# The first transfers of a retention-and-feed-forward kernel in another order: first weight piece behind two batches, one score and four state sums at other steps

**Chip, cores, metric.** One core of a Trainium2 chip. The metric is the device time of one execution in microseconds (us), the median of its runs.

## The reference

Retention over 4 batches, 8 heads, 768 steps and 64 dimensions, then a two-layer feed-forward block with leaky ReLU, all in fp32:

```python
state = gamma * state + einsum('bhd,bhe->bhde', k[:, :, t], v[:, :, t])
y[:, :, t] = scale * einsum('bhd,bhde->bhe', q[:, :, t], state)
...
h = x @ w_in            # x: 3072 x 512, w_in: 512 x 2048
g = np.maximum(0.01 * h, h)
return g @ w_out
```

The weights come as 64-bit words: ScalarE takes the powers of two out of a piece of 0.5 MB ("powers"), VectorE joins them with the mantissas in three operations ("mantissas"). Only then can TensorE multiply with that piece.

## The kernel before

The kernel works in chunks of 128 tokens of each of four batches. For chunk 0 each batch needs: its q/k (0.5 MB), scored by TensorE and masked by VectorE; its values v (0.25 MB), weighted by decays; the product of both ("values"); and VectorE's "taken", which writes x. `direct(...)` then multiplies x with the first four weight pieces in four steps. Fillers (`keep_busy`) are matmuls whose results nobody reads. Cut to what the change touches:

```python
load_qk(0, 0)
nc.sync.dma_start(out=dec[:, rates:], in_=decay[:, rates:])
load_piece(0)
load_qk(0, 1)
load_v(0, 0)
load_v(0, 1)
nc.sync.dma_start(out=dec[:, :rates], in_=decay[:, :rates])
load_piece(1)
load_qk(0, 2)
load_v(0, 2)
load_piece(2)
load_piece(3, ...)
load_qk(0, 3)
load_v(0, 3)
# ...
keep_busy(7)
score(0, 0)
masked(0, 0)
decay_v(0, 0)            # GpSimd
next_powers()
keep_busy(8)
score(0, 1)
masked(0, 1)
decay_v(0, 1)            # GpSimd
keep_busy(3)
values(0, 0)
next_mantissas()
values(0, 1)
taken(0, 0, x)
taken(0, 1, x)
next_powers()
keep_busy(3)
steps = direct(0, 0, x, parts[0][1], 0)
next(steps)              # first product with weights
score(0, 2)
next_mantissas()
# ... masked, decay_v(0, 2, nc.scalar), powers 2 and 3
next(steps)              # second product
# ... values(0, 2), score(0, 3), next(steps)
values(0, 3)
sums0 = two_banks("sums0")
first_state(0, sums0)
first_state(1, sums0)
# ... half of the next direct, then first_state(2), (3), first_states_taken
```

## Time and profile before

| | before |
|---|---|
| median of 6 runs, us | 671.26 (670.68 to 671.58) |
| span of the profiled run, us | 669.4 |
| TensorE busy | 661.8 us, 99% |
| first product with weights starts | 14.89 us |
| second product starts | 17.85 us |
| next chunk's first score starts | 30.45 us |
| first output product ("A_o") starts | 62.45 us |

The last four rows are starts in the time-ordered instructions of TensorE. From the first product on TensorE has no gap, so these starts are the measure: a start that moves earlier by some tenth moves the end by as much.

### The profile page before, as it was taken

Reading aid. Unit: us, or ns where it says so; the run is one execution under the profiler, and the core shown is the slowest. Engines: PE = TensorE matmul, PEld = TensorE weight load, DVE = VectorE, ACT = ScalarE, POOL = GpSimd, SP = SyncE. Lnnn points to the kernel's source line nnn. Section 1 sums busy time; section 2 is a strip of 40 time slices with the busy share of each in tenths; the row PEclk is TensorE's granted clock in tenths of the full one; section 3 lists DMA queues with packets and bytes.
Section 4 is the critical chain, followed back from the end, with each engine's and each line's share of the span. In section 5 each row is a group of like instructions: output and inputs, shape, how many; then the busy total and the mean of one; then the engine's idle time right before and its main releaser. Section 6 shows DMA issues by size and latency. Waiting matters only on the chain.

```text
span 669.4 us, 10422 instructions
## 1 busy us (share of the span) xinstructions
PE 661.8 (99%) x4517; PEld 573.9 (86%) x4517; DVE 368.3 (55%) x563; ACT 174.2 (26%) x319; POOL 21.4 (3%) x23
## 2 busy tenths in 40 slices
PE   7999999999999999999999999999999999999997
PEld 4888888888888888888888888888888888888886
DVE  4878769889889675414642623553531444331342
ACT  4754456255252002210301310210211220221210
POOL 1000000000000111000000100100100000000000
PEclk9999999999999999999999999999999999999999
DMA  8922222321411553003002200301300000000001
GB/s 323 401 81 95 69 88 64 94 95 63 158 64 64 189 190 127 1 0 112 17 16 80 95 0 1 126 1 64 126 1 0 2 0 34 29 1 1 0 1 63
DMA packets 16028, 49.16 MB, mean 73 GB/s; under 512 B 1904, under 2 KB 2160, under 8 KB 15984
## 3 DMA queue, kind: packets, MB, share of 16 engines
q1 hardware_dynamic: 15984, 48.51, 20.6%
q8 instruction: 35, 0.57, 0.4%
q14 instruction: 9, 0.07, 0.0%
HBM read 42.21 MB, written 6.29 MB: 72 GB/s over the span
## 4 chain that ended last, share of the span: by engine, by line
PE 97%; DMA 1%; DVE 0%; issue 0%; SPq 0%; DVEq 0%
PE B_o L389 12%; PE A_o L389 12%; PE C_o L389 12%; PE C_h L389 12%; PE B_h L389 12%; PE A_h L389 11%; PE D_o L389 6%; PE D_h L389 6%; PE d L411 4%; PE ap L165 3%; PE yp L193 3%; PE yp L184 2%; PE yp L208 1%; DMA qk<-in_qk_dram 1%; PE sums L208 0%
## 5 line engine op out<-in xcount | busy, mean ns | idle before, releaser
L389 PE MATMUL A_h<-x,w 128*128 128x256 f32 x352 | 83.2, 379 | 0.0
L389 PEld LDWEIGHTS A_h<-x,w 128*128 128x128 f32 x352 | 66.9, 190 | 9.1
L389 PE MATMUL A_o<-g,w 128*128 128x256 f32 x288 | 68.0, 379 | 0.0
L424 ACT ACTIVATE g<-g 128x512 f32<-128x512 f32 x66 | 40.2, 630 | 86.9 <-DVE g L338 86.9
L389 PEld LDWEIGHTS A_o<-g,w 128*128 128x128 f32 x288 | 54.7, 190 | 7.4
L429 ACT COPY m<-A_h 128x512 f32<-128x512 f32 x22 | 12.8, 583 | 139.4 <-PE A_h L389 100.5
L338 DVE TENSOR_TENSOR m<-m,B_o 128x512 f32<-128x512 f32 x16 | 11.0, 685 | 65.9 <-PE B_o L389 65.9
L338 DVE TENSOR_TENSOR m<-m,B_h 128x512 f32<-128x512 f32 x22 | 15.1, 686 | 56.8 <-PE B_h L389 56.8
L232 DVE TENSOR_TENSOR x<-yp,dec 128x512 f32<-128x512 f32 x24 | 16.4, 688 | 47.9 <-PE yp L208 35.6
L389 PE MATMUL C_h<-t,w 128*128 128x256 f32 x176 | 42.2, 383 | 0.0
L389 PE MATMUL B_h<-x,w 128*128 128x256 f32 x176 | 42.2, 383 | 0.0
L389 PE MATMUL B_h<-t,w 128*128 128x256 f32 x176 | 41.6, 379 | 0.0
L389 PE MATMUL C_h<-x,w 128*128 128x256 f32 x176 | 41.6, 379 | 0.0
L389 PE MATMUL D_h<-t,w 128*128 128x256 f32 x176 | 41.6, 379 | 0.0
L170 DVE TENSOR_TENSOR am<-ap,mask 128x1024 f32<-128x1024 f32 x24 | 28.6, 1221 | 16.1 <-PE ap L165 16.1
L389 PEld LDWEIGHTS C_h<-t,w 128*128 128x128 f32 x176 | 32.9, 190 | 5.3 <-issue 1.0
L389 PEld LDWEIGHTS B_h<-t,w 128*128 128x128 f32 x176 | 33.4, 190 | 4.5
L389 PEld LDWEIGHTS C_h<-x,w 128*128 128x128 f32 x176 | 33.4, 190 | 4.5
L389 PEld LDWEIGHTS D_h<-t,w 128*128 128x128 f32 x176 | 33.4, 190 | 4.5
L389 PEld LDWEIGHTS B_h<-x,w 128*128 128x128 f32 x176 | 32.9, 190 | 4.9 <-issue 0.3
L147 POOL TENSOR_TENSOR kv<-kv,dec 128x512 f32<-128x512 f32 x18 | 20.9, 1165 | 461.9 <-DMA kv<-in_kv_dram 263.6
L341 DVE TENSOR_TENSOR gd<-g,gd 128x512 f32<-128x512 f32 x48 | 34.7, 723 | 1.8
(109 smaller groups left out, 1056.2 us busy)
## 6 DMA issues: line engine op xcount, KB each, us to landing
raw<-in_weights_dram SPq DMA_DIRECT2D x31, 512.0 KB, 3.9
qk<-in_qk_dram SPq DMA_DIRECT2D x19, 512.0 KB, 4.4
kv<-in_kv_dram SPq DMA_DIRECT2D x17, 512.0 KB, 5.0
out_dram<-o SPq DMA_DIRECT2D x23, 256.0 KB, 2.1
in<-in_qk_dram SPq DMA_DIRECT2D x3, 512.0 KB, 7.2
in<-in_kv_dram SPq DMA_DIRECT2D x3, 512.0 KB, 7.8
kv<-in_kv_dram SPq DMA_DIRECT2D x4, 256.0 KB, 7.5
o_in<-in_qk_dram SPq DMA_DIRECT2D x2, 512.0 KB, 8.4
```

Of the source, the lines that this page charges most:

```text
L147: engine.tensor_tensor(out=v, in0=v, in1=gk.unsqueeze(2).to_broadcast([128, H, D]), op=ALU.mult)
L165: nc.tensor.matmul(ps[ts(u, 64), j, a, :], lhsT=x[ts(j, 64), 1, a, ts(u, 64)], rhs=x[ts(j, 64), 0, a, :])
L170: nc.vector.tensor_tensor(out=am.rearrange("p j a t -> p (j a) t"), in0=scores[c, b].rearrange("p j a t -> p (j a) t"), in1=mask.unsqueeze ...
L184: nc.tensor.matmul(ps[ts(i, 64), j, m, :], lhsT=st[b][ts(j, 64), a, :], rhs=x[ts(j, 64), 0, a, :], start=(m == 0), stop=False, skip_group_ ...
L193: nc.tensor.matmul(ps[ts(i, 64), j, m, :], lhsT=y[:, 1, 2 * a + j, :], rhs=am[:, j, a, :], start=(c == 0 and m == 0), stop=True, skip_grou ...
L232: nc.vector.tensor_tensor(out=blocks, in0=ps[:, :, 0 : HP // 2, :], in1=gq, op=ALU.mult)
L338: nc.vector.tensor_tensor(out=out, in0=a, in1=b, op=ALU.add)
L341: nc.vector.tensor_tensor(out=out, in0=a, in1=b, op=ALU.subtract)
L389: nc.tensor.matmul(half, lhsT=block(w, sa)[:, k, ts(i, 128)], rhs=rhs[:, k, :], start=(first and (i == 0 or split) and n == 0 and k == 0), ...
L411: nc.tensor.matmul(banks[r][:, i, :], lhsT=block(2 * u, r + 2 * kh)[:, k, ts(i, 128)], rhs=x[:, 2 * kh + th, k, :], start=(step == 0 and i ...
L424: nc.scalar.activation(g[:, i], g[:, i], AF.Prelu, alpha=0.01)
L429: nc.scalar.copy(out=got["m1"], in_=ps)
```

## The change

Intent: the q/k and values of the first two batches get in front of the first weight piece, so that more of TensorE's useful work fits into the time before the first product; the two decays of these batches go from GpSimd to VectorE; the third batch's score moves ahead of the first product; the four state sums come together.

```diff
     load_qk(0, 0)
     nc.sync.dma_start(out=dec[:, rates:], in_=decay[:, rates:])
+    load_v(0, 0)
+    load_qk(0, 1)
+    nc.sync.dma_start(out=dec[:, :rates], in_=decay[:, :rates])
+    load_v(0, 1)
     load_piece(0)
-    load_qk(0, 1)
-    load_v(0, 0)
-    load_v(0, 1)
-    nc.sync.dma_start(out=dec[:, :rates], in_=decay[:, :rates])
-    load_piece(1)
     load_qk(0, 2)
     load_v(0, 2)
+    load_piece(1)
     load_piece(2)
 ...
-    decay_v(0, 0)
-    next_powers()
-    keep_busy(8)
+    decay_v(0, 0, nc.vector)
+    keep_busy(6)
     score(0, 1)
+    values(0, 0)
     masked(0, 1)
-    decay_v(0, 1)
+    decay_v(0, 1, nc.vector)
     keep_busy(3)
-    values(0, 0)
+    next_powers()
+    taken(0, 0, x)
+    values(0, 1)
+    taken(0, 1, x)
+    next_powers()
     next_mantissas()
-    values(0, 1)
-    taken(0, 0, x)
-    taken(0, 1, x)
-    next_powers()
+    score(0, 2)
     keep_busy(3)
     steps = direct(0, 0, x, parts[0][1], 0)
     next(steps)
-    score(0, 2)
     next_mantissas()
+    decay_v(0, 2, nc.scalar)
 ...
+    sums0 = two_banks("sums0")
+    for b in range(B):
+        first_state(b, sums0)
     next_mantissas()
     load(1, 3)
     values(0, 3)
-    sums0 = two_banks("sums0")
-    first_state(0, sums0)
-    first_state(1, sums0)
 ...
     taken(0, 3, x)
+    first_states_taken(sums0)
 ...
-    first_state(2, sums0)
-    first_state(3, sums0)
-    first_states_taken(sums0)
```

The diff is cut to transfers and calls; the bookkeeping of tiles in the helper of the state sums moved with them. ScalarE's own order does not change by this: the third batch's decays stood between the powers of pieces 1 and 2 before as well.

More of the change, by code (lines that the diff above doesn't have):

```diff
@@ L212, in first_state @@
     def first_state(b, ps):
-        y = heads.pop((0, b))[1]
+        y = heads[0, b][1]
         sp = ps[:, b // 2].rearrange("p a t -> p (a t)")[:, ds(b % 2 * HP * D, HP * D)]
@@ L220, in first_states_taken @@
     def first_states_taken(ps):
+        for b in range(B):
+            heads.pop((0, b))
         flat = ps.rearrange("p j a t -> p (j a t)").rearrange("p (ba d) -> p ba d", d=D)
@@ L606 @@
     masked(0, 0)
-    decay_v(0, 0)
-    next_powers()
-    keep_busy(8)
-    score(0, 1)
-    masked(0, 1)
-    decay_v(0, 1)
-    keep_busy(3)
-    values(0, 0)
-    next_mantissas()
+    decay_v(0, 0, nc.vector)
+    keep_busy(6)
+    score(0, 1)
+    values(0, 0)
+    masked(0, 1)
+    decay_v(0, 1, nc.vector)
+    keep_busy(3)
+    next_powers()
+    taken(0, 0, x)
     values(0, 1)
-    taken(0, 0, x)
     taken(0, 1, x)
     next_powers()
+    next_mantissas()
+    score(0, 2)
     keep_busy(3)
@@ L622 @@
     next(steps)
-    score(0, 2)
     next_mantissas()
+    decay_v(0, 2, nc.scalar)
     load(1, 2, unit_tile(LATE[0], "in12"))
     masked(0, 2)
-    decay_v(0, 2, nc.scalar)
     next_powers()
@@ L633 @@
     score(0, 3)
-    decay_v(0, 3, nc.scalar)
     taken(0, 2, x)
     masked(0, 3)
+    decay_v(0, 3, nc.scalar)
     next(steps)
+    sums0 = two_banks("sums0")
+    for b in range(B):
+        first_state(b, sums0)
     next_mantissas()
```

## The prediction

> **What bounds the kernel now.** I read the page first (busy shares and the slices), then the chain that ended last in order of time, then the time-ordered instructions of TensorE, of VectorE and ScalarE and of the DMA-issuing queue over the first 35 us, and the waits of TensorE after the start. The page:
>
> ```profile
> span 669.4 us, 10422 instructions
> PE 661.8 (99%) x4517; PEld 573.9 (86%) x4517; DVE 368.3 (55%) x563; ACT 174.2 (26%) x319; POOL 21.4 (3%) x23
> ...
> PE   7999999999999999999999999999999999999997
> ...
> PEclk9999999999999999999999999999999999999999
> ```
>
> TensorE is busy for 99% of the span at full clock, and only the first and last slice are short of it. The TensorE waits from 14.89 us to the end of the span give one entry, and that is the one that ends at 14.89 us itself. So from there on TensorE does not stop, and no change in the first 35 us can gain more than the idle time before it, unless it removes work. The chain in order of time shows what those first microseconds wait for (start, length, what):
>
> ```profile
> 2.18 6.81 DMA qk<-in_qk_dram
> ...
> 9.03 1.15 PE ap L165 x32
> ...
> 11.34 0.79 DVE w L330
> ...
> 13.56 1.29 DVE x L232 x2
> 14.85 0.04 issue
> 14.89 1.99 PE d L411 x8
> 16.89 1.03 PE ap L165 x32
> 17.92 1.92 PE d L411 x8
> ```
>
> The second batch's q and k land at 8.98, its scores are made and masked, the first weight piece is put together on VectorE (L330 to L334), the two batches' values are taken into x, and the first product with weights ("d") starts at 14.89. TensorE in those 15 us, in order of time (the last bracket is idle time before the group):
>
> ```profile
> 4.39 1.10 PE L165 MATMUL ap<-qk 64*64 64x128 f32 x32
> 5.43 1.90 PE L601 MATMUL idle<-t 128*128 128x512 bf16 x8
> 9.03 1.10 PE L165 MATMUL ap<-qk 64*64 64x128 f32 x32 [1.70 <-DMA qk<-in_qk_dram]
> 10.06 0.82 PE L601 MATMUL idle<-t 128*128 128x512 bf16 x3
> 10.88 2.10 PE L193 MATMUL yp<-am,kv 128*64 128x128 f32 x32
> 12.91 0.82 PE L601 MATMUL idle<-t 128*128 128x512 bf16 x3
> 14.89 1.99 PE L411 MATMUL d<-x,w 128*128 128x256 f32 x8 [1.16 <-DVE x L232]
> ```
>
> Useful work before 14.89 is two scores and two values, some 4.2 us; the rest is idle or the deliberate filler of L601. The DMA issues show when transfers land. The queue holds eight in flight, so the issue of one from the ninth on begins as the one eight before it lands:
>
> ```profile
> 7.72 0.33 SPq L279 DMA_DIRECT2D raw<-in_weights_dram  x1
> 9.00 0.33 SPq L279 DMA_DIRECT2D x_words<-in_weights_dram  x1
> 9.66 0.33 SPq L131 DMA_DIRECT2D o_in<-in_qk_dram  x1
> 10.33 0.33 SPq L134 DMA_DIRECT2D o_in<-in_kv_dram  x1
> ```
>
> These four follow the landings of piece 0 (1.0 MB asked for by then), the second q/k (1.5 MB), the first values (1.75) and the second values (2.0). From here on the landings lie on a line: 7.72 us at 1.0 MB and 2.56 us for each MB more. The second piece (2.75 MB) landed at 12.25 and the third batch's q/k (3.25 MB) at 13.55, where the line gives 12.20 and 13.48. The queue is saturated, so a transfer's landing is set by the bytes in front of it.
>
> **What the Trainium skill says.** "DMA: Bandwidth & Descriptors", Queues, rings and completion order: descriptors on one engine are consumed in ring order. The line above agrees; moving a transfer forward makes those it passes later. "ScalarE: Activation LUTs", What ACT_TABLE_LOAD costs: an ACTIVATE takes 186 ns, plus about 93 for a pointer operand, plus 0.833 ns for each element, and neighbours overlap by 93. For 64 elements with a pointer scale that gives 332 ns, or eight in about 2.0 us; the trace has 333 ns each and 2.02 us for eight. "GPSIMD Engine Reference", Engine selection: a two-input elementwise operation is about twice as slow there as on VectorE. The trace has 1.04 us on GpSimd for the 128x512 decay and 0.68 to 0.69 us for VectorE operations of that size. "TensorE: Matmul & The Clock Gate", Part 1: The HAM clock gate: the clock halves after an idle window of about 3.4 us. The longest idle stretch here is 1.70 us, and the granted clock reads 1.00 in every stretch. No run here shows a throttle.
>
> **The change part by part.** It removes no useful instruction; two fillers of 21 go.
>
> 1. Transfers. In the new order the bytes asked for up to and including each are: first q/k 0.5 MB, first values 0.75, second q/k 1.25, query decays 1.5, second values 1.75, piece 0 2.25, third q/k 2.75, third values 3.0, piece 1 3.5, piece 2 4.0, piece 3 4.5, fourth q/k 5.0 as before. On the line: second q/k 8.36 (0.6 earlier), second values 9.64, piece 0 10.92 (3.2 later), third q/k 12.2 (1.3 earlier), piece 1 about 14.15 (1.9 later). All from piece 2 on are where they were.
>
> 2. First product. TensorE scores the second batch from 8.4. In the trace a mask starts 1.17 us after its score and holds VectorE for 1.14, giving 9.57 to 10.71. The second decay, now on VectorE, ends 0.68 later, near 11.4. The second batch's values take 1.1 and end at 12.55; its taking frees VectorE after 0.61, at 13.2. The four steps of VectorE's order that were ahead are done by then. Only now come the three operations of piece 0, which took 1.93 us from the first's start to the last's end for the second piece (14.76 to 16.69). They end at 15.13; ScalarE's powers of piece 0 (10.95 to 13.0) do not hold them. The first product starts at about 15.15, 0.26 **later** than before. But the third batch's score (1.03 us) has moved in front of it, into 12.6 to 13.6, where TensorE would idle. If nothing else bound it, the gain would be 1.03 - 0.26 = 0.77.
>
> 3. Second product. It needs piece 1: landing 14.15, ScalarE's first two powers 1.42 (12.28 to 13.67 in the trace, plus the hand-over), VectorE's three 1.93, hand-over 0.05: 17.55. TensorE would be ready at 15.15 + 1.93 = 17.08, so it waits some 0.45 us. The second product started at 17.85 before, with the same work behind it in both orders (values of batch three, score four, the other products and sums). The gain is therefore 17.85 - 17.55 = **0.30 us**, whatever the exact start of the first product.
>
> 4. ScalarE's decays of the third batch, between the powers of pieces 1 and 2. Powers 1 free it at 16.1, eight decays 1.92, powers 2 from 18.05, its second operation done at 19.45, VectorE's three done at 21.4. TensorE asks for piece 2 at 17.55 + 1.92 + 1.03 + 1.03 = 21.53. It just fits, with 0.1 us over. The third batch's values ask for their decays at 19.5 and have them at 18.05.
>
> 5. The state sums. All four batches now come together in front of the fourth batch's values, 23.5 to 25.5; the fourth batch's decays are done at about 23.9 (powers 3 end at 21.9, then 2.0), while its sum comes at 25.0. The PSUM pair needed by the next chunk's first score is free when VectorE has scaled the states, about 28.3; the score comes at 30.1. No wait. VectorE masks it perhaps 0.7 us later than before, at 32.4, but its values are read only at 37. The same TensorE work in another order: nothing gained or lost.
>
> Sum: 671.22 - 0.30 = **670.9 us**.
>
> **The rivals.** A: the whole moved score counts, and the start is not later. If piece 1's path is quicker than I reckon, the gain is 0.8 to 1.0 us: 670.3. For it: TensorE had 1.16 us idle just there. Against: the second piece is asked for 0.75 MB later in a saturated queue, which costs 1.9 us of landing, and the old path had only some 1.1 us of slack (its VectorE work ended at 16.69 for a product that started at 17.85). B: waits at each of the next pieces, because ScalarE is now full from 14.2 to 26 (powers, decays, powers, powers, decays, decays) and piece 2 has only 0.1 us over. A slip of 0.4 to 0.6 there eats the gain: 671.2 to 671.6. For it: ScalarE shows hardly a gap here before, and the decays come before the powers of pieces 2 and 3. Against: ScalarE's durations are steady within a few ns. C: the second q/k does not land earlier, because the start of the DMA stream, 4.2 to 7.7 us, is not yet on the line. Then the first product starts at 15.75 and the second at 17.7: gain 0.15, 671.1. D: TensorE's clock drops in the idle stretch near 7 to 8.4, with six fillers in place of eight. The stretch is 1.5 us, shorter than the 1.70 us of before, so I hardly believe it; it would cost 1 to 2 us.
>
> **Range and chances.** My central 670.9 stands on the landing of piece 1. A gives 670.3, B up to 671.6. The three runs before spread over 0.9 us (670.68 to 671.58), more than the effect, so the range is 670.1 to 671.7. Two per cent would be 13.4 us. TensorE has only 7.6 us without work in the whole span, so faster by that much is out of reach; slower by it would need a stall of many microseconds that no dependence shows. Chances: faster 0.01, same 0.98, slower 0.01.
>
> **What would show each step right or wrong.** Second q/k landing near 8.4 and its score starting there (step 1). First product at about 15.15, with the third score already done and the last wait before it on VectorE's work for piece 0 (step 2). A new TensorE wait of 0.3 to 0.6 us before the second product, at 17.55, behind VectorE's piece work (step 3). No wait longer than 0.2 us before the third product at 21.5 (step 4). No wait at the sums, and the next chunk's first score at about 30.15 against 30.45 (step 5). The prediction is wrong if TensorE has a wait anywhere after 22 us, if the sum of the waits after the first product is over 0.8 us, or if the second product starts before 17.2.

## The result, and the profile after

Changed: median **670.87 us** of 6 runs (670.45 to 671.16); before: 671.26 of 6. The ratio is 0.9994, 95% interval 0.9981 to 1.0007: the same, by this measure. (Ratios are the mean time of one kernel's fast runs over that of the other's of the same rounds, so not quite the ratio of the medians.)

The head of the changed kernel's page:

```profile
span 668.9 us, 10414 instructions
...
PE 662.3 (99%) x4515; PEld 574.3 (86%) x4515; DVE 370.7 (55%) x565; ACT 174.1 (26%) x319; POOL 19.0 (3%) x21
```

GpSimd has two instructions fewer and VectorE two more: the two decays. Next, TensorE in order of time (start, length, what; the last bracket is idle time before the group and what ended it):

```profile
8.27 1.10 PE L165 MATMUL ap<-qk 64*64 64x128 f32 x32 [0.39 <-DMA qk<-in_qk_dram]
...
12.44 1.10 PE L165 MATMUL ap<-o_in 64*64 64x128 f32 x32
13.47 0.82 PE L603 MATMUL idle<-t 128*128 128x512 bf16 x3
15.15 1.99 PE L413 MATMUL d<-x,w 128*128 128x256 f32 x8 [0.85 <-DVE w L336]
17.46 1.99 PE L413 MATMUL d<-x,w 128*128 128x256 f32 x8 [0.31 <-DVE w L336]
```

The third score now lies at 12.44, ahead of the first product, which starts 0.26 us later than before. Before the second product there is a wait of 0.31 us that was not there, and still it starts 0.39 us earlier (17.46 against 17.85). All waits of TensorE over the whole span (waiter, what it waited for, total, times, longest):

```profile
PE idle L603 <- DVE t L598: 1.4, 1, 1.4
PE d L413 <- DVE w L336: 1.2, 2, 0.9
PE ap L165 <- DMA qk<-in_qk_dram: 0.4, 1, 0.4
PE yp L193 <- DVE kv L147: 0.3, 1, 0.3
```

No wait comes after 17.46. The chain that ended last has changed its beginning (start, length, what):

```profile
5.82 8.25 DMA raw<-in_weights_dram
...
14.10 0.67 ACT w L320
...
15.45 0.44 DVE w L332
...
16.71 0.70 DVE w L336
...
17.46 1.99 PE d L413 x8
```

Before, it ran over the second batch's q/k and the first product. Now it runs over **piece 1**: its transfer, ScalarE's powers, VectorE's three operations, the second product. The marks:

| start of, us | before | after | earlier by |
|---|---|---|---|
| first product | 14.89 | 15.15 | -0.26 |
| second product | 17.85 | 17.46 | 0.39 |
| next chunk's first score | 30.45 | 29.91 | 0.54 |
| A_o | 62.45 | 61.91 | 0.54 |

The lines of the last two rows, before and then after:

```profile
30.45 1.10 PE L165 MATMUL ap<-in 64*64 64x128 f32 x32
...
62.45 1.89 PE L389 MATMUL A_o<-g,w 128*128 128x256 f32 x8
```

```profile
29.91 1.10 PE L165 MATMUL ap<-in 64*64 64x128 f32 x32
...
61.91 1.89 PE L391 MATMUL A_o<-g,w 128*128 128x256 f32 x8
```

So 0.39 us comes before the second product, and 0.15 between it and the next chunk. The spans agree: 669.4 - 668.9 = 0.5 us. These are marks of one trace each; two more traces of the changed kernel follow, and they differ from it.

### The profile page after: what moved, and what is told of

The parts are those of the page before. It is cut to its first block, busy times and chain, and to the rows that moved or that the text cites. A ratio compares the mean times of both kernels' runs of the same rounds, so it can differ in the third digit from the quotient of the medians.

```text
span 668.9 us, 10414 instructions
## 1 busy us (share of the span) xinstructions
PE 662.3 (99%) x4515; PEld 574.3 (86%) x4515; DVE 370.7 (55%) x565; ACT 174.1 (26%) x319; POOL 19.0 (3%) x21
## 4 chain that ended last, share of the span: by engine, by line
PE 97%; DMA 1%; SPq 1%; DVE 0%; ACT 0%; issue 0%; DVEq 0%
PE B_o L391 12%; PE A_o L391 12%; PE C_o L391 12%; PE B_h L391 12%; PE C_h L391 12%; PE A_h L391 11%; PE D_o L391 6%; PE D_h L391 6%; PE d L413 4%; PE yp L193 3%; PE ap L165 3%; PE yp L184 2%; DMA raw<-in_weights_dram 1%; PE yp L208 1%; PE sums L208 0%; SPq L131 0%
## 5 line engine op out<-in xcount | busy, mean ns | idle before, releaser
L343 DVE TENSOR_TENSOR gd<-g,gd 128x512 f32<-128x512 f32 x48 | 36.3, 756 | 1.8
L391 PE MATMUL C_o<-gd,w 128*128 128x256 f32 x144 | 34.0, 379 | 0.0
```

The costliest lines, as they stand in the source:

```text
L343: nc.vector.tensor_tensor(out=out, in0=a, in1=b, op=ALU.subtract)
L391: nc.tensor.matmul(half, lhsT=block(w, sa)[:, k, ts(i, 128)], rhs=rhs[:, k, :], start=(first and (i == 0 or split) and n == 0 and k == 0), ...
```

## The experiments

Twelve runs. Single looks give a trace each; the marks are read from them. All results were correct.

**Do the marks repeat?** The kernel before and the changed kernel, once more, unedited.

> Control: the kernel before, once more, to see how well one trace repeats. The marks are the start of the first and second product with weights (14.89 and 17.85 us), the next chunk's first score (30.45) and the first output product A_o (62.45). Expected within 0.1 us of these, if the DMA landings repeat as the durations do. If they move by 0.3 us or more, none of the differences here can be read from single traces.

> Control: the changed kernel once more. Marks of the first trace: first score 1.99 us long at 4.49, first product 15.15, second 17.46, next chunk's first score 29.91, A_o 61.91. Expected within 0.1 us; the length of the first score may differ (1.10 or 1.99), since the clock of TensorE is just coming up there, and if it does, the rest should not move.

The kernel before repeated: 14.84, 17.79, 30.39, 62.40, all within 0.06 us. The changed kernel did **not**: 15.46, 19.09, 31.54, 63.54, and 672.32 us. Its ScalarE and TensorE lines of the time-ordered views:

```profile
15.72 0.67 ACT L320 ACTIVATE w<-raw 128x512 f32<-128x512 uint16 x1 [2.55 <-DMA raw<-in_weights_dram]
```

```profile
19.09 1.99 PE L413 MATMUL d<-x,w 128*128 128x256 f32 x8 [1.63 <-DVE w L336]
```

Piece 1's powers start at 15.72 in place of 14.10, 1.62 us later; the second product follows 3.37 us after, where it was 17.46 - 14.10 = 3.36 in the first trace. So the mechanism held and the landing moved. My expectation that single traces repeat to 0.1 us was wrong for this kernel; what follows is therefore read from differences inside one trace where possible.

**Does piece 1's landing set the second product?** Piece 1 with 0.25 MB less in front of it, then with 0.5 MB more:

```diff
     load_qk(0, 2)
+    load_piece(1)
     load_v(0, 2)
-    load_piece(1)
     load_piece(2)
```

```diff
     load_qk(0, 2)
     load_v(0, 2)
+    load_piece(2)
     load_piece(1)
-    load_piece(2)
```

> The changed kernel with the transfers of piece 1 and of the third batch's values exchanged, so that piece 1 has 0.25 MB less in front of it. My theory (piece 1's landing sets the second product): piece 1 lands at 13.45 in place of 14.1, the second product follows the first without a wait at 17.08, A_o 0.38 us earlier, near 61.53. Rival (VectorE's queue or ScalarE's sets it and the landing is hidden): the second product stays at 17.4 to 17.5 and A_o at 61.9.

> The changed kernel with the transfers of pieces 1 and 2 exchanged, so that piece 1 has 0.5 MB more in front of it. My theory: piece 1 lands at 15.4 in place of 14.1, the second product starts at 18.75 with a wait of 1.6 us before it, and all after shifts by 1.3 us: A_o near 63.2. Rival (the landing is hidden behind the first product and ScalarE): under 0.5 us later.

Early: piece 1's powers start at 13.02, the wait is gone, both products run in one stretch, A_o at 61.06 (expected 61.53; 0.40 of the difference is that the second q/k was scored at 7.87 and not at 8.27 in this run). Late: powers at 15.04, second product at 18.41 after a wait of 1.60, A_o at 62.86 (expected wait 1.6, A_o 63.2; the stream was some 0.35 us earlier as a whole). TensorE of both, early and late:

```profile
14.75 3.85 PE L413 MATMUL d<-x,w 128*128 128x256 f32 x16 [0.85 <-DVE w L336]
```

```profile
14.81 1.99 PE L413 MATMUL d<-x,w 128*128 128x256 f32 x8 [0.86 <-DVE w L336]
18.41 1.99 PE L413 MATMUL d<-x,w 128*128 128x256 f32 x8 [1.60 <-DVE w L336]
```

The same first product, and only the wait behind it differs. The rival, that the landing is hidden, is out.

**Does VectorE's load ahead of the first product matter?** The two decays back on GpSimd:

```diff
-    decay_v(0, 0, nc.vector)
+    decay_v(0, 0)
 ...
-    decay_v(0, 1, nc.vector)
+    decay_v(0, 1)
```

> The changed kernel with the first two batches' decays back on GpSimd. If the second product's start hangs on piece 1 alone, the first product may come 0.2 to 0.3 us earlier (VectorE has 0.6 us less to do ahead of piece 0, and the second values can be decayed as they land, at 9.6) while the second product stays at 17.46 and A_o at 61.9. Rival (VectorE's load ahead of the first product is what the end hangs on): A_o 0.2 to 0.3 us earlier too. Third possibility (GpSimd and VectorE slow one another): VectorE operations beside GpSimd's grow, and the first product comes later than 15.15.

The first product came at 14.80, 0.35 us earlier; the second at 17.44 and A_o at 61.89, as in the first trace of the change (17.46, 61.91). What the first product gained, the wait for piece 1 took (0.64 us in place of 0.31). Beside GpSimd's decays only a mask and the start of a taking ran on VectorE, and they kept their length (1.22 and 0.68 us). So in the changed kernel the move of the decays to VectorE is neither gain nor loss for the end. The third possibility is not out for other operations: in both traces of the kernel before, the first operation of piece 0's mantissas (L330, at 11.34 and 11.28) ran beside GpSimd's second decay and took 0.78 us, where every later run of it in the first 60 us took 0.42. There it lay on the way to the first product; no experiment separates this.

**Are the four sums together worth something?** The sums back at their two old steps:

```diff
-    for b in range(B):
-        first_state(b, sums0)
     next_mantissas()
     load(1, 3)
     values(0, 3)
+    first_state(0, sums0)
+    first_state(1, sums0)
 ... (2 and 3, and first_states_taken, behind the next first step, as before)
```

> The changed kernel with the state sums at their old steps, two batches behind the fourth values and two behind the first product of the second half. The trace after the change shows 12.45 us of TensorE from the second product to the next chunk's first score, against 12.60 before, with the same matmuls. If the grouping of the four sums saves it (fewer turns from one shape of matmul to another): next chunk's score 0.15 us later than 29.91 and A_o near 62.05. If the prediction was right that grouping is neutral: 29.91 and 61.9.

This run met two accidents, a late piece 1 (powers at 15.74) and a half clock (its second product took 3.40 us and not 1.99; more on this below), and A_o at 65.34 says nothing. But the stretch from the third product to the next chunk's first score is free of both:

| stretch, us | sums split | sums together |
|---|---|---|
| third product to next score | 8.62 before, 8.61 its second trace, 8.61 here (24.73 to 33.34), 8.61 with the transfers alone | 8.47 in each of the changed kernel's three traces, and in the early and late runs above |

The same matmuls take **0.14 us less** when the sums are in one block ahead of the fourth batch's values. That is the 0.15 found in the marks. Why is not shown: fewer turns from one shape of matmul to another would fit it, but the run moved the block as well as splitting it.

**Does the moved score pay?** The score back behind the first product:

```diff
     next_mantissas()
-    score(0, 2)
     keep_busy(3)
     steps = direct(0, 0, x, parts[0][1], 0)
     next(steps)
+    score(0, 2)
     next_mantissas()
```

> The changed kernel with the third batch's score put back behind the first product. My theory (the moved score fills a hole and is what pays): first product unchanged at 15.15, score 17.1 to 18.1, second product 18.1 in place of 17.46, its wait gone, and everything after 0.65 us later: A_o near 62.55, slower than before the change by 0.1. Rival (the gain comes from the earlier q/k and the grouped sums, the score's place is neutral because piece 1 is waited for anyway): A_o stays within 0.2 of 61.9.

A_o came at 63.92, far later than either expected. The reason is in TensorE's own lengths and in the windows view (busy time of each engine, then granted clock, DMA share, GB/s):

```profile
14.88 3.61 PE L413 MATMUL d<-x,w 128*128 128x256 f32 x8 [1.89 <-DVE w L336]
```

```profile
14.00:16.00 2.00, 1.12 (x3) 0.95 (x4) 1.49 (x4) 1.94 (x5) 0.00 (x0) 0.77 1.02 401
16.00:18.00 2.00, 2.00 (x6) 1.40 (x5) 1.04 (x2) 2.00 (x9) 0.00 (x0) 0.50 1.03 389
18.00:20.00 2.00, 2.00 (x36) 1.37 (x35) 0.39 (x1) 1.94 (x4) 0.00 (x0) 0.87 1.06 395
```

After 1.89 us without work TensorE ran at half clock for about 3.4 us (means of 0.77, 0.50 and 0.87 over two microseconds each make 0.92, 2.0 and 0.52 us at half), and the first product took 3.61 us and not 1.99.

The clock records of the traces, read directly, show more. In this run the clock was full from 4.85 us, half from 15.09 to 18.51, and full again: the half lasted 3.41 us and began three times 3.41 after the first record. In "sums back" it was full from 5.88 and half from 19.54 to 22.95: again 3.41, after four times 3.41. I cut every trace into stretches of 3.41 us from its first record and summed TensorE's matmuls in each. Ahead of the two drops they are 1.52 us (11.68 to 15.09 here) and 1.54 us (16.12 to 19.53 in "sums back"). The next lowest are 1.78 (16.04 to 19.45 in the change's second trace) and 1.98 ("piece 1 late"), and the clock stayed full; no other stretch of the 14 traces had less than 2 us. So in these traces the work in such a stretch decided, and not the length of the gap alone. With two drops, all that is known of the limit is that it lies between 1.54 and 1.78 us of 3.41.

So the run mixed two things: the place of the score and the clock. I split them with eight fillers in the hole in place of three:

```diff
-    keep_busy(3)
+    keep_busy(8)
     steps = direct(0, 0, x, parts[0][1], 0)
     next(steps)
     score(0, 2)
```

> The changed kernel with the third batch's score back behind the first product, as in the earlier run, but with eight fillers in place of three in the hole that it leaves. In that earlier run the first product came after 1.9 us without work and ran at half clock (3.61 us in place of 1.99). Theory: the fillers hold the clock, the first product is 1.99 us long again, and the second starts 2.96 us after the first (1.93 and 1.03): if the first is at 15.0, the second at 17.95 and A_o, 44.45 later, at 62.4, some 0.5 later than the changed kernel in its first trace. That is what the moved score itself is worth. Rival (the lost clock has another cause than the idle stretch): the first product is again longer than 2.5 us.

```profile
14.85 1.99 PE L413 MATMUL d<-x,w 128*128 128x256 f32 x8 [0.81 <-DVE w L336]
16.78 1.10 PE L165 MATMUL ap<-o_in 64*64 64x128 f32 x32
17.81 1.99 PE L413 MATMUL d<-x,w 128*128 128x256 f32 x8
```

Full clock, first product at 14.85, second 2.96 later at 17.81, A_o at 62.27. In this run piece 1's powers started at 13.82; with the score ahead, the second product could have started 3.37 later, at 17.19, so the moved score is worth 17.81 - 17.19 = 0.62 us in it (an estimate from the other traces' 3.37). In the run at half clock the same sum gives 13.84 + 3.37 = 17.21 against 14.88 + 1.93 + 1.03 = 17.84: 0.63, as expected (0.65), and the clock cost 19.47 - 17.84 = 1.63 us on top. The rival, that the score's place is neutral, is out.

**The transfers without the rest.** The kernel before, with the new order of the first eleven transfers only:

```diff
     # as in the change: v0, second q/k, query decays, v1, piece 0, third q/k, v2, piece 1
```

> The kernel before with the new order of transfers alone. My theory: piece 0 lands at 10.9, its three VectorE operations run 12.25 to 14.2, then the two takings, so the first product starts near 15.45; the score stays behind it, and the second product starts near 18.4 (15.45 + 1.93 + 1.03), later than the 17.85 of before: A_o near 63.0, slower by 0.55. So the transfers alone lose and only pay with the moved score. Rival (earlier q/k of batches two and three is itself the gain): A_o under 62.45.

First product 15.07, second 18.03, A_o 62.63: 0.18 us later than before (expected 0.55; the powers of piece 0 started at 10.47 in this run, where the expectation took 10.9, which covers the miss of 0.37). The new order by itself gives nothing; in this change it pays by having the third q/k there early enough for the third score.

One rival was not run: the **score moved alone**, in the old order of transfers. In the trace of the kernel before, the third q/k had landed at 13.55, TensorE was idle from 13.73 to 14.89, and piece 1's VectorE work ended at 16.69. An estimate from these numbers: the score fits into the hole, and the second product starts at 14.89 + 1.93 = 16.82, 1.03 us earlier than before, where the change got 0.39. The last experiment below supports it: its third q/k has the same 3.25 MB asked for as in the kernel before, and its score still lies ahead of the first product. So that the score needed the third q/k ahead of piece 1 is not shown, and likely wrong.

**Why did the repeat slip?** The trace also lists single DMA packets. Up to 22 us each trace has one packet of the instruction queue, 16 KB, which takes 1.1 us; I put its time on the axis of the page by matching the bytes moved in each half microsecond. All eight traces with the change's transfer order:

```
run             powers of piece 0   of piece 1   apart   instruction packet at
change, first         10.87           14.10      3.23          14.9
score back            10.58           13.84      3.26          14.6
decays on GpSimd      10.84           14.07      3.23          14.3
transfers alone       10.47           13.71      3.24          14.6
score back, fill      10.57           13.82      3.25          14.7
change, third         10.90           14.46      3.56          12.1
change, second        11.17           15.72      4.55          12.6
sums back             10.96           15.74      4.78          12.4
```

Where the packet came after piece 1 had landed, the two pieces are 3.23 to 3.26 us apart; where it came before, 3.56, 4.55 and 4.78. Five against three fit, but it is an observation: I could not move the packet, and why it comes at 12 or at 14 to 15 is open. Outside the table one trace does not fit: with piece 1 early, the packet came near 11.8, before piece 1 landed at 13.0, and the pieces were 2.56 apart, as in its second trace (2.57, packet near 15.6). So an early packet does not always make piece 1 late, and the cause of the late landings is not shown. I timed the changed kernel again to see how often it costs:

> The changed kernel timed again. In all five traces in which piece 1 bound it, the second product started 3.40 us after piece 1 landed, but the landing was 14.1 in two of them and 15.7 in two others of the same transfer order, where a 16 KB instruction fetch came at 12.2 to 12.5 and not at 14.2 to 14.8. If that is right, the runs of this kernel come in two groups some 1.5 us apart, near 670.8 and 672.3, while the kernel before stays in one. If the late run was a stray of the chip: one group near 670.8.

One group: 670.17 to 670.97, median 670.72, against 671.14 (670.80 to 671.67) for the kernel before in the same rounds; ratio 0.9990 (0.9977 to 1.0003). The two groups that I expected are not there. Its profiled run even had an early packet, with 0.3 us of delay only; its second product started at 17.83 and A_o at 62.28. So of twelve executions of the changed kernel one (672.32) was late; how often that happens stays open. The changed kernel's three traces have A_o at 61.91, 62.28 and 63.54, against 62.45 and 62.40 before: the 0.54 us of the first trace is the best of them. By time the medians are 0.4 us apart in both sets of runs (671.26 to 670.87, 671.14 to 670.72), and both intervals leave room for no gain at all.

**Better versions.** The kernel with piece 1 early, timed, and one that takes all findings: pieces 0 and 1 in front of the third q/k, piece 0 put together before the second "taken", the fillers ahead of the third score.

```diff
     load_piece(0)
+    load_piece(1)
     load_qk(0, 2)
     load_v(0, 2)
-    load_piece(1)
 ...
     values(0, 1)
+    next_mantissas()
     taken(0, 1, x)
     next_powers()
-    next_mantissas()
-    score(0, 2)
     keep_busy(3)
+    score(0, 2)
```

> The kernel with piece 1 in front of the third batch's values, timed. Theory: as VectorE and not the landing binds the second product there, 0.4 to 0.8 us faster than the changed kernel's usual runs, near 670.1, and with fewer or smaller late runs. Rival (the one run at 669.66 was luck of the start of the stream): near 670.8 as the changed kernel.

> Pieces 0 and 1 both in front of the third batch's q/k, piece 0 put together before the second batch's values are taken, and the three fillers ahead of the third score in place of behind it. Theory: piece 1 lands at 12.3 with 0.6 us of slack, first product near 14.4 (VectorE's three operations fill its wait for the second values), second near 16.35 with no wait over 0.1, A_o near 60.8: about 1.6 us faster than before the change and 1.1 faster than the change, near 669.7, and one group of runs. Rival (the third score, whose q/k now land at 13.0, or something behind it becomes the wait): first product at 14.9 or later and A_o over 61.3.

Piece 1 early: 670.02 us (669.57 to 670.59), ratio 0.9984 (0.9970 to 0.9998). In its profiled run, too, both products run in one stretch, from 15.07, with A_o at 61.38, so the first trace was not luck. Pieces first: **669.82 us** (669.35 to 669.97), ratio 0.9977 (0.9964 to 0.9990). Both intervals lie under 1, if barely for the first; the means are 0.16 and 0.23 per cent lower, which is still "same" by the measure of 2%. The second version changes three things at once, which of them pays is not separated, and that it beats the first is not shown. TensorE of the latter:

```profile
13.14 1.10 PE L165 MATMUL ap<-o_in 64*64 64x128 f32 x32 [0.34 <-DMA o_in<-in_qk_dram]
14.44 3.85 PE L413 MATMUL d<-x,w 128*128 128x256 f32 x16 [0.19 <-DVE x L234]
```

The products start at 14.44 and run without a wait, A_o at 60.75 (expected 14.4 and 60.8), 1.70 us earlier than before.

## Why the prediction was right

- **The sum.** 670.9 predicted, 670.87 measured; "same". The agreement to 0.03 us is luck: run times spread over 0.7 us, the prediction started from the median of three runs (671.22), and its gain of 0.30 left out parts that the first trace shows (steps 3 and 5; 0.54 in all). The marks are the better test.
- **Step 1, transfers.** The line of landings gave 8.36, 10.92 and 14.15; scored or powered at 8.27, 10.87 and 14.10. In the later traces the line's start moved between 7.87 and 8.59: rival C, that the start of the stream is not on the line, names a real spread; the prediction priced it as one shift (671.1), and not as something that differs from run to run.
- **Step 2, first product.** 15.15 predicted, 15.15 seen, and the third score lay in the hole as said. The exact hit is in part luck too: the second score came 0.13 us earlier than reckoned, and VectorE's last step for piece 0 only 0.04 (15.09 for 15.13).
- **Step 3, second product.** 17.55 and a wait of 0.45 predicted; 17.46 and 0.31 seen. The cause is shown by the early and late runs, and 3.36 or 3.37 us from the powers to the product in six traces (the first trace, its two repeats, piece 1 late, decays on GpSimd, sums back). The term was 0.09 too small: gain 0.39, not 0.30. Rival A, the whole score as gain, failed for the reason given. The landing itself is less steady than the step had it: in the second trace the wait was 1.63 us, over the 0.8 that the prediction named as a sign against it, and in the third 0.64.
- **Step 4, ScalarE.** As said, no wait before the third product (21.44 in the first trace; 21.53 asked for, less the 0.09). Rival B did not happen there.
- **Step 5, the sums.** "The same TensorE work in another order: nothing gained or lost" was **wrong by 0.14 us**: the block of four takes less than two blocks of two, in every trace that has it. It had no wait, as said; the mis-sized term is TensorE's own time. With it the gain in the traces is 0.39 + 0.14 = 0.53, near the 0.54 seen, where 0.30 was predicted.
- **Rival D, the clock.** "I hardly believe it" was too sure, and the statement that the trace of before shows no throttle was wrong: its first seven fillers took 0.44 us each, against 0.24 for the eight later ones (1.90 us, shown in the prediction), so TensorE started slow, though the clock column read 1.00. The first clock record of that trace is at 4.23 us, of full clock (6.37 in the first trace of the change); ahead of it the column has nothing to read. The line of TensorE in order of time, kernel before:

```profile
1.40 3.07 PE L601 MATMUL idle<-t 128*128 128x512 bf16 x7 [1.40 <-DVE t L596]
```

In the first trace of the change the first score took 1.99 us and not 1.10 for the same reason (4.49 to 6.41, up to that first record); nothing hung on it, as the second score waited for its q/k after it (0.39 us). The loss that rival D described, 1 to 2 us after an idle stretch, did come in two experiments (1.63 us in one), ahead of the products and not at 7 to 8.4. The change itself was not seen to suffer it; in its late run it waited 1.63 us at full clock.

## What to carry to other kernels

In a saturated queue, bytes moved forward push others back: after such a change, look for the next consumer of what was passed, and for how much slack it had (here 17.85 - 16.69 = 1.16 us, of which nothing was left). Before moving transfers to make room for a piece of work, look whether the room is there already: here the score might have moved alone. An order that leaves no slack before a transfer also shows the chance events of the queue, so repeat its trace before believing one; measure by starts of stages when the whole time spreads more than the effect. When an experiment opens a hole on TensorE, check the lengths of its matmuls behind it, and fill the hole, as the eight fillers did here, to keep the clock out of the comparison.

## What the Trainium skill lacked or had wrong

- "TensorE: Matmul & The Clock Gate", The HAM clock gate and HAM oscillation: it warns of gaps over about 3.4 us. Here gaps of 1.89 us (score back) and 1.86 us (sums back) were followed by half clock for some 3.4 us, while 1.92 us (transfers alone) and 1.63 us (the change's second trace) were not. A gap of little more than half the named length can do it. The page's free-running window of that length agrees with the clock records (half clock for 3.41 us, at whole multiples of 3.41 from the first record), but the window need not be idle: 1.52 and 1.54 us of matmuls in it did not hold the clock, and 1.78 did.
- The same page on the slow start agrees with the fillers (0.44 us, then 0.24), but no page says that the profile's clock column can read 1.00 during it, where the trace has no clock record yet (none before 4.23 us in the kernel before).
- "DMA: Bandwidth & Descriptors", Queues, rings and completion order: it says that an engine takes turns between queue rows, and not what an instruction fetch then costs a load. The page that treats instruction fetches ("Runtime: NRT & Kernel Launch", Instruction fetch mechanics) does not say it either. Here one 16 KB packet took 1.1 us; piece 1 was 0.3 to 1.5 us late in three traces that had it early, and not late in a fourth, so what it costs stays open.
- "GPSIMD Engine Reference", Engine selection: about twice as slow for two inputs; here 1.04 us against 0.68 for the same 128x512 decay, 1.5 times.
- No page has what splitting a group of small matmuls costs: here 0.14 us for the state sums in two blocks and not one, the reason not shown.
